# Batch 0's softmax division moved from ScalarE to VectorE and POOL, with new gates on the loads, in a fused attention and squared-ReLU kernel

## The chip, the cores and the metric

The kernel runs on one core of a Trainium2 chip. The metric is the device time of one execution in microseconds. Before the change three runs gave 326.56, 328.07 and 330.91, median 328.07.

## The reference, cut to what matters

```python
scores = scale * np.matmul(q, k.transpose(0, 1, 3, 2))     # B, H, S, D = 4, 8, 768, 64
# mask: own block of 32 and its neighbours, first and last block, 3 sampled blocks a row
scores = np.where(mask, scores, -1000000000.0)
scores = scores - np.max(scores, axis=-1, keepdims=True)
attn = np.exp(scores)
attn = attn / (np.sum(attn, axis=-1, keepdims=True) + 1e-09)
attn_out = np.matmul(attn, v)
x = attn_out.transpose(0, 2, 1, 3).reshape(B * S, H * D)    # 3072 tokens x 512
h = x @ w_in                                                # 512 x 2048
r = np.maximum(h, 0.0)
out = (r * r) @ w_out                                       # 2048 x 512
```

## The kernel before, in words

**Units, slots, groups.** The attention is cut into 16 units `u`, a unit being one pair of heads of one batch (4 units a batch). A unit has 3 query blocks `qi` of 256 queries, and each of them 3 key chunk pairs `cp` of 256 keys. One (u, qi, cp) is a *slot*: TensorE makes the transposed scores of both heads in a PSUM tile `ps` (line 360), ScalarE takes exp into `pT` in bf16 (line 366), and TensorE multiplies `pT` with the values (lines 384 and 386) into `po`. The value tiles `VA` and `VB` carry 64 columns of ones, so that `po` holds the outputs of a head in one half of its partitions and the sums of exp in the other half. The three slots of one (u, qi) are a *group*; there are 48. `po` has one buffer, and so the values of the next group wait until the last reader of the group before is done.

**The division (lines 389 to 405).** After a group's last slot ScalarE takes Ln of the two halves with the sums and Exp of minus that (`inverse`, `ls` and `rs`), and VectorE multiplies outputs and reciprocals into `xT`, one product for each half (`normalize`). These two products are the last readers of `po`.

**The mask.** In batch 0 (u < 4) it is added on TensorE ahead of the scores, as a product of one-hot rows `oh` and a table `bq` (line 356); `bq` comes from `bm`, which VectorE builds from `sampled_blocks` (`sb_i`) at the start, by a product `pb` and one copy of 128x768 on ScalarE (lines 271 to 278). From batch 1 on `pT` is multiplied on VectorE by a 0/1 table `mask` (line 371), which is made in nine pieces during batch 0 (`pq`, lines 280 to 290).

**The feed-forward part.** Batch 0 is worked in 3 tiles of 256 tokens, the others in 2 tiles of 384. For each of 16 blocks `f` of the hidden width TensorE makes `ph` (line 421), VectorE or ScalarE takes the ReLU (`relu_eng` decides; lines 430 and 432), POOL squares it (line 438), and TensorE multiplies with `w_out_sb` into `py` (line 451), which ScalarE copies out (line 456).

**Loads.** Q, K and V come over SP's queue. For batch 0 they are loaded in parts (line 175) and transposed on TensorE. For u of 4 and more, `load(u)` issues three DMAs (line 164), VectorE casts K and POOL casts Q (line 299), and SP issues two DMA transposes (line 321). The weights come over POOL's queue, cast on the way: four pieces of `w_in` (line 335) and four of `w_out` (line 338). A tiny DMA that reads a piece of `w_in` (`loads_gate`, line 342) holds SP's queue until that piece has landed; behind it stand the loads of u = 4 and later.

**What sets the order.** Every engine runs its instructions in the order in which they were issued. That order is made on the host by `run_schedule` (lines 122 to 149): each piece of work is a `Task` with an engine, an assumed duration, a key and what it depends on; the planner takes the task that can start first by these durations, ties by key, and a task behind another on its engine waits with it. Durations, keys, `after` times and gates thus change nothing but the order.

Of the kernel before, what the change touches and what calls it, by code (L numbers as in the profile page):

```python
# [25 lines left out]
def kernel(  # L26
# [136 lines left out]
    def load_part(eng, u, w, c0, c1):  # L166
# [3 lines left out]
        if raw[u][w] is None:  # L170
# [4 lines left out]
        eng.dma_start(out=raw[u][w].rearrange("p t n d -> p t (n d)")[:, :, cols],  # L175
                      in_=(qv, kv, vv)[w][b, a][:, :, cols])

    load_part(nc.scalar, 0, 1, 0, 1)
    load_part(nc.sync, 0, 0, 0, 1)
    sb_i = consts.tile([nb, n_rand * 2], I32, name="sb_i")  # L180
    nc.scalar.dma_start(out=sb_i, in_=sampled_blocks.bitcast(I32))
    load_part(nc.sync, 0, 1, 1, CP)
    load_part(nc.sync, 0, 2, 0, CP)
    load_part(nc.sync, 1, 1, 0, CP)
# [18 lines left out]
    def init_v(eng, i):  # L203
        eng.memset(VA[i][:, :, D:P], 1.0)
        eng.memset(VB[i][:, :, 0:D], 1.0)
# [62 lines left out]
    mask = consts.tile([P, NQ, NCH, QW], BF, name="mask")  # L268
    mtile = {}

    def rows_product():
        pb = ps_s.tile([P, 1024], F32, name="pb", tag="ps")
        nc.tensor.matmul(pb[:, 0:512], bm, oh[0:nb, 0:512], start=True, stop=True)
        nc.tensor.matmul(pb[:, 512:S], bm, oh[0:nb, 512:S], start=True, stop=True)
        mtile["rows"] = pb

    def rows_copy():
        nc.scalar.copy(out=bq, in_=mtile.pop("rows")[:, 0:S])

    def mask_product(qi, cp):  # L280
        pq = ps_y.tile([P, 2, QW], F32, name="pq", tag="y")
# [55 lines left out]
            ns = slice((i - NWP) * NF // NWP, (i - NWP + 1) * NF // NWP)  # L337
            nc.gpsimd.dma_start(out=w_out_sb[:, ns, :], in_=wov[:, ns, :])

    def loads_gate():  # L340

        nc.sync.dma_start(out=scratch, in_=w_in_sb[0:1, 0, (NWP - 1) * d_ff // NWP:(NWP - 1) * d_ff // NWP + 1])


    ptile, stile, otile, rtile, xT = {}, {}, {}, {}, {}
# [1 line left out]
    def scores(slots):  # L347
        for u, qi, cp in slots:
            i = u % NPB
            ps = ps_s.tile([P, 2, 2, QW], F32, name="ps", tag="ps")  # L350
            qsl = slice(qi * QW, (qi + 1) * QW)
            ksl = [slice((cp * 2 + c) * P, (cp * 2 + c + 1) * P) for c in range(2)]
            add = u < HP
            for c in range(2 if add else 0):
                for h, hs in enumerate(HALVES):
                    nc.tensor.matmul(ps[:, h, c, :], oh[hs, ksl[c]], bq[hs, qsl], start=c == 0, stop=False,
                                     skip_group_check=True)
            for c in range(2):
                for h, hs in enumerate(HALVES):
                    nc.tensor.matmul(ps[:, h, c, :], KT[i][hs, ksl[c]], QT[i][hs, qsl], start=not add,  # L360
                                     stop=True, skip_group_check=True)
            stile[u, qi, cp] = ps
# [26 lines left out]
    def inverse(u, qi):  # L389
# [5 lines left out]
        nc.scalar.activation(out=rs, in_=ls, func=AF.Exp, scale=-1.0)  # L395
        rtile[u, qi] = rs

    def normalize(u, qi):
        b, a = divmod(u, HP)
        if b not in xT:  # L400
            xT[b] = consts.tile([P, HP, S], BF, name=f"xT{b}")
        po, rs = otile.pop((u, qi)), rtile.pop((u, qi))
        qsl = slice(qi * QW, (qi + 1) * QW)
        V.tensor_mul(out=xT[b][0:D, a, qsl], in0=po[0:D, 0, :], in1=rs[0:D, :])  # L404
        V.tensor_mul(out=xT[b][D:P, a, qsl], in0=po[D:P, 1, :], in1=rs[D:P, :])  # L405
# [16 lines left out]
                             start=(kc == 0), stop=(kc == KM - 1))  # L422

    def relu_eng(T, f):
        return "ACT" if f % 3 == 2 or (T[0] == 0 and T[1] and f % 3) else "DVE"

    def relu(T, f):
        r = work.tile([P, TWM], F32, name="r", tag="r", bufs=R_BUFS)[:, 0:T[2]]
# [40 lines left out]
            load_part(nc.sync, u, 0, c, c + 1)  # L469
    for i in range(HP):  # L470
        init_v(G, i)

    PT_BUFS, R_BUFS, G_BUFS, QC_BUFS = 9, 4, 2 * NF + 3, 5

    K_PARTS = {0: [(0, 1), (1, CP)]}
# [13 lines left out]
        sc_of[u], va_of[u] = [], []  # L489
    wl, tr, gate, mk, tp = {}, {}, [], {}, {HP - 1: []}  # L490

    rp = Task("PE", 0.5, -7, rows_product, get="ps", **pe)
    rc = Task("ACT", 0.8, -7, rows_copy, deps=[rp], put=[rp], **SEM)
    for qi in range(NQ):
        for cp in range(CP):
            s = HP * CP * NQ + qi * CP + cp - 16
            t = Task("PE", 0.27, s, (lambda a=(qi, cp): mask_product(*a)), deps=[rc],
                     get="y", after=20.0 + 3 * (qi * CP + cp), **pe)
            mk[qi, cp] = Task("DVE", 0.62, s, (lambda a=(qi, cp): mask_copy(*a)), deps=[t], put=[t], **SEM)

    def prepare_first(u):

        tr[u], ev[u] = [], {}
        parts = [(1, c0, c1, t, first[u]) for (c0, c1), t in zip(K_PARTS.get(u, [(0, CP)]), land_k[u])]
        parts += [(0, c, c + 1, land_q[u][c], c * HP * CP + first[u]) for c in range(CP)]
        for w, c0, c1, at, s in parts:
            n = c1 - c0
            a = (u, w, c0, c1)
            on = "POOL" if c0 and not w else "DVE"
            c = Task(on, 0.06 + (0.17 if on == "DVE" else 0.36) * n, s - 6,  # L510
                     (lambda a=a, e=G if on == "POOL" else V: cast_qk(e, *a)), get="qc", after=at, **SEM)
            t = Task("PE", 0.15 * n, s - 5 - w, (lambda a=a: transp(*a)), deps=[c], get="h", put=[c], **pe)
            e = Task("DVE", 0.06 + 0.17 * n, s - 5, (lambda a=a: evac(*a)), deps=[t], put=[t], **SEM)
            tr[u].append(c)
            for i in range(c0, c1):
                ev[u][w, i] = e
        cv[u] = [Task("POOL", 0.6, first[u] - 2, (lambda u=u, h=h: cast_v(u, h)), after=land_v[u], **SEM)
                 for h in range(2)]
        if u == HP - 2:

            for i in range(NWP):
                wl[i] = Task("POOL", 1.0, first[u] + i, (lambda i=i: w_load(i)), deps=cv[u], late=2.0,
                             dma=3.4)
            gate.append(Task("SP", 0.5, 0, loads_gate, deps=[wl[NWP - 1]], late=0.0))

    def prepare(u):
        s0 = first[u]

        ld_t = Task("SP", 1.3, s0 - 20, (lambda u=u: load(u)), deps=cv[u - NRAW] + tr[u - NRAW] + gate,
                    late=2.0, dma=3.9, behind=tp[u - 1])  # L530
        old_sc = sc_of[u - NPB] if u >= NPB else []
        old_va = va_of[u - NPB] if u >= NPB else []
        tr[u], ev[u], tp[u] = [], {}, []
        for w in (1, 0):
            c = Task("DVE" if w else "POOL", 0.6 if w else 1.2, s0 - 12,
                     (lambda w=w: cast_qk(V if w else G, u, w, 0, CP)), deps=[ld_t], get="qc", **SEM)
            t = Task("SP", 1.5, s0 - 12, (lambda w=w: transp_dma(u, w)), deps=[c] + old_sc, put=[c],
                     late=2.0, dma=1.5)
            tr[u].append(c)
            tp[u].append(t)  # L540
            for i in range(CP):
                ev[u][w, i] = t
        early = []
        if u < NPB:
            early = [Task("POOL", 0.8, s0 - 8, (lambda u=u: init_v(G, u)), after=36.0, **SEM)]
        cv[u] = [Task("POOL", 0.6, s0 - 12, (lambda u=u, h=h: cast_v(u, h)), deps=[ld_t] + old_va + early, **SEM)
                 for h in range(2)]
        if u == HP:
            for i in range(NWP, 2 * NWP):
                wl[i] = Task("POOL", 1.0, s0 - 12 + i, (lambda i=i: w_load(i)), deps=cv[u], late=2.0, dma=4.5)  # L550

    N_FIRST = HP * NQ * CP
    N_ONE = 72

    def attend(s, slots):
        sc = Task("PE", 0.42 if len(slots) == 1 and s >= N_FIRST else 0.645, s, (lambda: scores(slots)),
                  deps=[rc] + [ev[u][1, cp] for u, qi, cp in slots] + [ev[u][0, qi] for u, qi, cp in slots] + sc_all[-1:],
                  get="ps", n=len(slots), **pe)
        sc_all.append(sc)
        for j, a in enumerate(slots):  # L560
            u, qi, cp = a
            k = s + j
            ex = Task("ACT", 0.97, k, (lambda a=a: exps(*a)), deps=[sc], get="pT", put=[sc.bufs[j]], **SEM)
            mm = ex
            if u >= HP:
                mm = Task("DVE", 0.82, k - 1, (lambda a=a: mask_mul(V, *a)), deps=[ex, mk[qi, cp]], **SEM)
            va = Task("PE", 0.44, k + 2.2, (lambda a=a: values(*a)), deps=[mm] + cv[u] + va_all[-1:],
                      get=None if cp else "po", put=[ex], **pe)
            va_all.append(va)
            sc_of[u].append(sc)  # L570
            va_of[u].append(va)
            if cp == CP - 1:
                inv = Task("ACT", 1.2, k - 9, (lambda u=u, qi=qi: inverse(u, qi)), deps=[va], **SEM)
                mu[u, qi] = Task("DVE", 0.87, k - 9, (lambda u=u, qi=qi: normalize(u, qi)), deps=[inv],
                                 put=[va_all[-CP]], **SEM)
# [15 lines left out]
    for k, T in enumerate(TILES + [None]):  # L591
# [4 lines left out]
        for _, kind, x in sorted(both, key=lambda e: e[:2]):  # L596
# [15 lines left out]
            else:  # L612
# [9 lines left out]
                if part == NY - 1:  # L622
# [1 line left out]
                              put=[yhead], **SEM)  # L624
                    Task("SP", 0.5, 0, (lambda T_=T_, ts=ts: store(T_, ts)), deps=[yc], put=[yc], late=2.0)

    run_schedule({"PE": 4.9, "DVE": 4.8, "ACT": 3.5, "POOL": 7.5, "SP": 10.5},
                 {"ps": 2, "po": 1, "h": 2, "y": 1, "pT": PT_BUFS, "r": R_BUFS, "g": G_BUFS, "ys": 3,
                  "qc": QC_BUFS}, ring={"SP": 16.0, "POOL": 14.0})

# [29 lines left out]
```

## Time and profile before

| | us |
|---|---|
| median of three runs | 328.07 |
| the profiled execution, its own time | 330.83 |
| its span in the trace | 329.0 |
| TensorE busy (matmuls) | 308.1 |
| ScalarE busy | 229.3 |
| VectorE busy | 197.9 |
| POOL busy | 172.4 |
| mean granted TensorE clock | 0.995 |

A row of a timeline gives the start, the duration, the engine, the line, the operation, what it writes and reads, and in square brackets how long the engine had been idle and what ended that. A row of the waits gives who waited, for whom, the total, the number of waits and the longest. The table of stages gives for each stretch the busy time of each engine and its number of instructions. SPq is SP's DMA queue.

### The profile page before, as it was taken

The page shows a single profiled execution, that of the slowest core. Times are in us where ns is not written, and L with a number is a line of the kernel's source. Part 1 is how long each engine was busy: PE and PEld are TensorE (multiplying, and loading weights), DVE is VectorE, ACT ScalarE, POOL GpSimd, SP SyncE. Part 2 cuts the span into 40 slices and gives each one's busy share as a digit, 9 for nine tenths or more (in the row PEclk, how much of TensorE's full clock was granted, in tenths as well). Part 3 has the DMA queues.
Part 4 walks back from the last instruction along what each step waited for, and adds up shares of the span by engine and source line. Part 5 has one row for each costly group of instructions (what it writes and reads, how often), then busy time and mean ns, then how long its engine had stood idle before and what let it go on. Part 6 is the DMA issues. An engine that isn't in the chain of part 4 may idle for free. (4 is left out here: it accounts for less than half of the span.)

```text
span 329.0 us, 6118 instructions
## 1 busy us (share of the span) xinstructions
PE 308.1 (94%) x2299; PEld 173.8 (53%) x2332; DVE 197.9 (60%) x358; ACT 229.3 (70%) x369; POOL 172.4 (52%) x226
## 2 busy tenths in 40 slices
PE   7989893999999999899999999999999999999994
PEld 2645452655555555455555655555555555555541
DVE  7443542268788687578787775788776764332200
ACT  2799982789799998778787789888778963211111
POOL 7550532287577635178968550356554343665620
PEclk9999999899999999999999999999999999999999
DMA  7997598635563674656061300000000000000002
GB/s 217 335 210 168 106 180 224 181 75 174 169 180 84 194 187 113 192 176 191 2 172 53 81 36 32 2 32 2 32 34 0 33 34 33 34 32 32 34 32 96
DMA packets 42451, 34.47 MB, mean 105 GB/s; under 512 B 20662, under 2 KB 39350, under 8 KB 42422
## 3 DMA queue, kind: packets, MB, share of 16 engines
q1 hardware_dynamic: 37890, 29.76, 31.5%
q0 software_dynamic: 4224, 4.19, 8.0%
q8 instruction: 18, 0.29, 0.4%
q10 hardware_dynamic: 308, 0.13, 0.1%
q14 instruction: 11, 0.09, 0.1%
HBM read 27.26 MB, written 6.29 MB: 102 GB/s over the span
## 5 line engine op out<-in xcount | busy, mean ns | idle before, releaser
L438 POOL TENSOR_TENSOR g<-r 128x384 bf16<-128x384 f32 (+1 forms) x144 | 127.7, 896 | 103.9 <-DVE r L432 76.4
L366 ACT ACTIVATE pT<-ps 128x1024 bf16<-128x1024 f32 x144 | 143.1, 1021 | 37.4 <-PE ps L360 24.1
L421 PE MATMUL ph<-xT,w_in_sb 128*128 128x384 bf16 (+1 forms) x576 | 116.5, 309 | 0.8 <-ACT r L430 0.2
L451 PE MATMUL py<-w_out_sb,g 128*128 128x512 bf16 x351 | 100.5, 379 | 3.6 <-ACT ys L456 2.1
L371 DVE TENSOR_TENSOR pT<-pT,mask 128x1024 bf16<-128x1024 bf16 x108 | 87.1, 820 | 23.7 <-ACT pT L366 21.9
L384 PE MATMUL po<-pT,VA 128*128 128x256 bf16 x288 | 72.3, 278 | 8.5 <-DVE xT L405 5.7
L421 PEld LDWEIGHTS <-w_in_sb 128*128 128x128 bf16 x576 | 53.0, 98 | 44.3 <-issue 10.8
L432 DVE TENSOR_SCALAR r<-ph 128x384 f32<-128x384 f32 (+1 forms) x89 | 46.3, 523 | 49.1 <-PE ph L421 34.4
L386 PE MATMUL po<-pT,VB 128*128 128x256 bf16 x288 | 71.8, 276 | 0.0
L451 PEld LDWEIGHTS <-g 128*128 128x128 bf16 x384 | 37.3, 98 | 27.9 <-issue 2.7
L360 PE MATMUL ps<-QT,KT 64*128 64x256 bf16 x576 | 50.9, 276 | 0.1
L384 PEld LDWEIGHTS <-VA 128*128 128x128 bf16 x288 | 28.2, 98 | 33.8 <-issue 16.8
L430 ACT ACTIVATE r<-ph 128x384 f32<-128x384 f32 (+1 forms) x55 | 23.9, 438 | 26.5 <-POOL g L438 15.9
L360 PEld LDWEIGHTS <-KT 64*128 64x128 bf16 x576 | 22.7, 95 | 20.7 <-issue 18.7
L386 PEld LDWEIGHTS <-VB 128*128 128x128 bf16 x288 | 28.4, 99 | 5.8
L404 DVE TENSOR_TENSOR xT<-po,rs 64x256 bf16<-64x256 f32 x48 | 19.8, 413 | 16.0 <-ACT rs L395 14.8
L299 POOL CAST qc<-qs 128x768 bf16<-128x768 f32 (+1 forms) x20 | 14.4, 727 | 21.1 <-DMA qs<-in_q_dram 19.1
L393 ACT ACTIVATE ls<-po 64x256 f32<-64x256 f32 x48 | 18.3, 382 | 9.9 <-PE po L386 8.9
L456 ACT COPY ys<-py 128x512 f32<-128x512 f32 x24 | 13.9, 584 | 15.2 <-PE py L451 11.4
L395 ACT ACTIVATE rs<-ls 128x256 f32<-128x256 f32 x48 | 20.0, 418 | 1.5
L405 DVE TENSOR_TENSOR xT<-po,rs 64x256 bf16<-64x256 f32 x48 | 20.5, 428 | 0.6
L304 POOL CAST VA<-vs 128x384 bf16<-128x384 f32 x16 | 10.3, 642 | 17.1 <-PE po L384 11.1
(51 smaller groups left out, 112.5 us busy)
## 6 DMA issues: line engine op xcount, KB each, us to landing
vs<-in_v_dram SPq DMA_DIRECT2D x16, 384.0 KB, 5.0
out_dram<-ys SPq DMA_DIRECT2D x24, 256.0 KB, 2.0
ks<-in_k_dram SPq DMA_DIRECT2D x15, 384.0 KB, 4.3
qs<-in_q_dram SPq DMA_DIRECT2D x12, 384.0 KB, 3.6
w_in_sb<-in_moe_w_in_dram POOLq DMA_DIRECT2D x4, 512.0 KB, 9.8
w_out_sb<-in_moe_w_out_dram POOLq DMA_DIRECT2D x4, 512.0 KB, 11.1
qs<-in_q_dram SPq DMA_DIRECT2D x12, 128.0 KB, 6.0
ks<-in_k_dram SPq DMA_DIRECT2D x1, 256.0 KB, 3.3
```

Source lines behind the costliest of these rows:

```text
L360: nc.tensor.matmul(ps[:, h, c, :], KT[i][hs, ksl[c]], QT[i][hs, qsl], start=not add, stop=True, skip_group_check=True)
L366: nc.scalar.activation(out=pT, in_=stile.pop((u, qi, cp)), func=AF.Exp, scale=scale)
L371: eng.tensor_mul(out=pT, in0=pT, in1=mask[:, None, qi, cp * 2:cp * 2 + 2, :].broadcast_to([P, 2, 2, QW]))
L384: nc.tensor.matmul(po[:, 0, :], VA[i][:, n, :], pT[:, 0, c, :], start=first, stop=last, skip_group_check=True)
L386: nc.tensor.matmul(po[:, 1, :], VB[i][:, n, :], pT[:, 1, c, :], start=False, stop=last, skip_group_check=True)
L395: nc.scalar.activation(out=rs, in_=ls, func=AF.Exp, scale=-1.0)
L405: V.tensor_mul(out=xT[b][D:P, a, qsl], in0=po[D:P, 1, :], in1=rs[D:P, :])
L421: nc.tensor.matmul(ph, w_in_sb[:, kc, f * P:(f + 1) * P], xT[b][:, kc, c0:c0 + w], start=(kc == 0), stop=(kc == KM - 1))
L430: nc.scalar.activation(out=r, in_=htile.pop((T, f)), func=AF.Relu)
L432: V.tensor_scalar(out=r, in0=htile.pop((T, f)), scalar1=0.0, scalar2=None, op0=AOP.max)
L438: G.tensor_mul(out=g, in0=r, in1=r)
L451: nc.tensor.matmul(py, gtile[T, f][:, ts * P:(ts + 1) * P], w_out_sb[:, f, :], start=(f == 0), stop=(f == NF - 1))
```

## The change

- At the start `sb_i` is loaded first on SP's queue; the first parts of K and of Q of unit 0 both go over ScalarE's queue.
- The table `bq` is made in three pieces of 256 columns, each with a product of its own in the `y` PSUM buffer and a copy of its own on ScalarE.
- The pieces of `mask` are made in another order and earlier by their keys.
- In batch 0 the 12 groups are divided in another way: four VectorE copies take outputs and sums out of `po` into `ls` and `rs` (`unload`), POOL raises the sums to the power -1 (a tile of -1 as second operand) and multiplies (`divide`). Batches 1 to 3 stay as they were.
- A second gate: after all of `w_out` has landed (u = 5 and later). The first gate reads the last column of `w_in`. The load of u = 5 need no longer stand behind the transposes of u = 4.
- ReLU: the first tile all on VectorE; in the other two tiles of batch 0 every second block on ScalarE (before: two in three); no change in batches 1 to 3.
- Some of the planner's numbers.

`NQ_ADD` is 3, which is `NQ`, so that the additive mask is used where it was before.

```diff
+    sb_i = consts.tile([nb, n_rand * 2], I32, name="sb_i")
+    nc.sync.dma_start(out=sb_i, in_=sampled_blocks.bitcast(I32))
     load_part(nc.scalar, 0, 1, 0, 1)
-    load_part(nc.sync, 0, 0, 0, 1)
-    sb_i = consts.tile([nb, n_rand * 2], I32, name="sb_i")
-    nc.scalar.dma_start(out=sb_i, in_=sampled_blocks.bitcast(I32))
+    load_part(nc.scalar, 0, 0, 0, 1)
...
-    def rows_product():
-        pb = ps_s.tile([P, 1024], F32, name="pb", tag="ps")
-        nc.tensor.matmul(pb[:, 0:512], bm, oh[0:nb, 0:512], start=True, stop=True)
-        nc.tensor.matmul(pb[:, 512:S], bm, oh[0:nb, 512:S], start=True, stop=True)
-        mtile["rows"] = pb
-
-    def rows_copy():
-        nc.scalar.copy(out=bq, in_=mtile.pop("rows")[:, 0:S])
+    def rows_product(qi):
+        pb = ps_y.tile([P, QW], F32, name="pb", tag="y")
+        nc.tensor.matmul(pb, bm, oh[0:nb, qi * QW:(qi + 1) * QW], start=True, stop=True)
+        mtile[qi] = pb
+
+    def rows_copy(qi):
+        nc.scalar.copy(out=bq[:, qi * QW:(qi + 1) * QW], in_=mtile.pop(qi))
...
-    def loads_gate():
-
-        nc.sync.dma_start(out=scratch, in_=w_in_sb[0:1, 0, (NWP - 1) * d_ff // NWP:(NWP - 1) * d_ff // NWP + 1])
+    def loads_gate(n):
+
+        last = w_in_sb[0:1, 0, d_ff - 1:d_ff] if n == 1 else w_out_sb[0:1, NF - 1, 0:1]
+        nc.sync.dma_start(out=scratch, in_=last)
...
-            add = u < HP
+            add = u < HP and qi < NQ_ADD
...
+    def unload(u, qi):
+
+        po = otile.pop((u, qi))
+        et = work.tile([P, QW], F32, name="ls", tag="ls")
+        st = work.tile([P, QW], F32, name="rs", tag="rs")
+        V.tensor_copy(out=et[0:D, :], in_=po[0:D, 0, :])
+        V.tensor_copy(out=st[0:D, :], in_=po[D:P, 0, :])
+        V.tensor_copy(out=et[D:P, :], in_=po[D:P, 1, :])
+        V.tensor_copy(out=st[D:P, :], in_=po[0:D, 1, :])
+        rtile[u, qi] = (et, st)
+
+    def divide(u, qi):
+        b, a = divmod(u, HP)
+        if b not in xT:
+            xT[b] = consts.tile([P, HP, S], BF, name=f"xT{b}")
+        et, st = rtile.pop((u, qi))
+        G.tensor_tensor(out=st, in0=st, in1=minus, op=AOP.pow)
+        G.tensor_mul(out=xT[b][:, a, qi * QW:(qi + 1) * QW], in0=et, in1=st)
...
-        return "ACT" if f % 3 == 2 or (T[0] == 0 and T[1] and f % 3) else "DVE"
+        return "ACT" if (T[0] and f % 3 == 2) or (T[0] == 0 and T[1] and f % 2) else "DVE"
...
+    minus = consts.tile([P, QW], F32, name="minus")
+    V.memset(minus, -1.0)
+
+    NQ_ADD = 3
...
-    rp = Task("PE", 0.5, -7, rows_product, get="ps", **pe)
-    rc = Task("ACT", 0.8, -7, rows_copy, deps=[rp], put=[rp], **SEM)
+    rc = []
+    for qi in range(NQ):
+        rp = Task("PE", 0.2, -7 + 7 * qi, (lambda qi=qi: rows_product(qi)), get="y", **pe)
+        rc.append(Task("ACT", 0.4, -7 + 7 * qi, (lambda qi=qi: rows_copy(qi)), deps=[rp], put=[rp], **SEM))
...
-            s = HP * CP * NQ + qi * CP + cp - 16
-            t = Task("PE", 0.27, s, (lambda a=(qi, cp): mask_product(*a)), deps=[rc],
-                     get="y", after=20.0 + 3 * (qi * CP + cp), **pe)
+            s = HP * CP * NQ_ADD + (qi - 2) % NQ * CP + cp - 6
+            t = Task("PE", 0.27, s, (lambda a=(qi, cp): mask_product(*a)), deps=[rc[qi]],
+                     get="y", after=13.0 + 2.5 * ((qi - 2) % NQ * CP + cp), **pe)
...
-            gate.append(Task("SP", 0.5, 0, loads_gate, deps=[wl[NWP - 1]], late=0.0))
+            gate.append(Task("SP", 0.5, 0, (lambda: loads_gate(1)), deps=[wl[NWP - 1]], late=0.0))
...
-        ld_t = Task("SP", 1.3, s0 - 20, (lambda u=u: load(u)), deps=cv[u - NRAW] + tr[u - NRAW] + gate,
-                    late=2.0, dma=3.9, behind=tp[u - 1])
+        ld_t = Task("SP", 1.3, s0 - 20, (lambda u=u: load(u)), deps=cv[u - NRAW] + tr[u - NRAW] + gate[-1:],
+                    late=2.0, dma=3.9, behind=tp[u - 1] if u > HP + 1 else [])
...
-                wl[i] = Task("POOL", 1.0, s0 - 12 + i, (lambda i=i: w_load(i)), deps=cv[u], late=2.0, dma=4.5)
+                wl[i] = Task("POOL", 1.0, s0 - 12 + i, (lambda i=i: w_load(i)), deps=cv[u], late=2.0, dma=4.0)
+            gate.append(Task("SP", 0.5, 0, (lambda: loads_gate(2)), deps=[wl[2 * NWP - 1]], late=0.0))
...
             if cp == CP - 1:
+                if u < HP:
+                    un = Task("DVE", 1.7, k - 9, (lambda u=u, qi=qi: unload(u, qi)), deps=[va],
+                              put=[va_all[-CP]], **SEM)
+                    mu[u, qi] = Task("POOL", 2.4, k - 9, (lambda u=u, qi=qi: divide(u, qi)), deps=[un], **SEM)
+                    continue
...
-    run_schedule({"PE": 4.9, "DVE": 4.8, "ACT": 3.5, "POOL": 7.5, "SP": 10.5},
+    run_schedule({"PE": 4.4, "DVE": 4.3, "ACT": 3.5, "POOL": 7.5, "SP": 10.5},
```

The diff shows the order only through its rules, so the rows that moved are shown here at two places on VectorE and SP/POOL, with the numbers of the buffers where rows would read alike.

**VectorE, the cast of K of unit 5.** This is the place in batch 0 where VectorE takes K of unit 5 (`ks_789` before, `ks_1230` now) into bf16. Before:

```order
L432 TENSOR_SCALAR r_861<-ph_847 128x256
L289 TENSOR_SCALAR mask_167<-pq_842 128x512
L299 CAST qc_919<-ks_789 128x768
L404 TENSOR_TENSOR xT0_377<-po_856,rs_904 64x256
L405 TENSOR_TENSOR xT0_377<-po_856,rs_904 64x256
L432 TENSOR_SCALAR r_945<-ph_923 128x256
```

Now:

```order
L422 TENSOR_TENSOR xT1_1259<-po_1266,rs_1299 64x256
L423 TENSOR_TENSOR xT1_1259<-po_1266,rs_1299 64x256
L450 TENSOR_SCALAR r_1332<-ph_1310 128x256
L297 CAST qc_1341<-ks_1230 128x768
L450 TENSOR_SCALAR r_1358<-ph_1343 128x256
```

The cast stood between batch 0's groups, ahead of the products of one of them (`xT0`); it now stands behind the second group of unit 4 (`xT1`), after all of batch 0's groups.

**POOL, the loads of `w_out`.** Before, behind the casts of V of unit 4:

```order
L299 CAST qc<-qs 128x768
L304 CAST VA_115<-vs 128x6x64
L304 CAST VB_116<-vs 128x6x64
L338 DMA w_out_sb<-in_moe_w_out_dram 128x4x512 x4
L438 TENSOR_TENSOR g<-r 128x256 x5
```

Now (L413 is the power, L414 the product of `divide`):

```order
L302 CAST VA_115<-vs 128x6x64
L302 CAST VB_116<-vs 128x6x64
L456 TENSOR_TENSOR g<-r 128x256
L413 TENSOR_TENSOR rs<-rs,minus 128x256
L414 TENSOR_TENSOR xT_390<-ls,rs 128x256
L336 DMA w_out_sb<-in_moe_w_out_dram 128x4x512 x2
L413 TENSOR_TENSOR rs<-rs,minus 128x256
L414 TENSOR_TENSOR xT_390<-ls,rs 128x256
L336 DMA w_out_sb<-in_moe_w_out_dram 128x4x512 x2
```

The four loads now stand behind a square and the seventh and eighth of the twelve divisions.

**SP's queue at the same place, now:**

```order
L319 DMA_TRANSPOSE QT_113<-qc 128x6x128
L319 DMA_TRANSPOSE KT_114<-qc 128x6x128
L341 DMA scratch<-w_out_sb 1x1
L163 DMA qs<-in_q_dram 128x2x384
L163 DMA ks<-in_k_dram 128x2x384
L163 DMA vs<-in_v_dram 128x2x384
```

The gate on `w_out` (`scratch`) is new; ahead of it are the transposes of unit 4, behind it the loads of unit 5. Before, those loads followed the transposes directly.

More of the change, by code (lines that the diff above doesn't have):

```diff
@@ L549, in prepare @@
             for i in range(NWP, 2 * NWP):
[L550 to L552 removed]
+                wl[i] = Task("POOL", 1.0, s0 - 12 + i, (lambda i=i: w_load(i)), deps=cv[u], late=2.0, dma=4.0)
+            gate.append(Task("SP", 0.5, 0, (lambda: loads_gate(2)), deps=[wl[2 * NWP - 1]], late=0.0))
+    N_FIRST = HP * NQ_ADD * CP
     N_ONE = 72
@@ L556, in attend @@
         sc = Task("PE", 0.42 if len(slots) == 1 and s >= N_FIRST else 0.645, s, (lambda: scores(slots)),
-                  deps=[rc] + [ev[u][1, cp] for u, qi, cp in slots] + [ev[u][0, qi] for u, qi, cp in slots] + sc_all[-1:],
+                  deps=[rc[qi] for u, qi, cp in slots if qi < NQ_ADD and u < HP] + [ev[u][1, cp] for u, qi, cp in slots] + [ev[u][0, qi] for u, qi, cp in slots] + sc_all[-1:],
                   get="ps", n=len(slots), **pe)
@@ L564, in attend @@
             mm = ex
-            if u >= HP:
+            if u >= HP or qi >= NQ_ADD:
                 mm = Task("DVE", 0.82, k - 1, (lambda a=a: mask_mul(V, *a)), deps=[ex, mk[qi, cp]], **SEM)
```

## The prediction

> **What bounds the kernel now.** First the busy times of the whole page, then the same by stages, since the shares of the whole are a mean over stages with different limits.
>
> ```profile
> span 329.0 us, 6118 instructions
> PE 308.1 (94%) x2299; PEld 173.8 (53%) x2332; DVE 197.9 (60%) x358; ACT 229.3 (70%) x369; POOL 172.4 (52%) x226
> ```
>
> ```profile
> core 0: us, PE busy (x) PEld busy (x) DVE busy (x) ACT busy (x) POOL busy (x), PEclk, DMA share, GB/s
> 16.00:48.00 32.00, 29.11 (x313) 16.80 (x311) 15.89 (x36) 29.06 (x42) 13.37 (x25) 1.00 0.93 166
> 48.00:60.00 12.00, 7.01 (x53) 3.90 (x53) 1.85 (x5) 5.09 (x8) 2.01 (x3) 0.87 0.89 203
> 60.00:72.00 12.00, 11.87 (x108) 6.97 (x109) 5.62 (x12) 10.04 (x18) 7.10 (x11) 0.99 0.40 118
> 72.00:120.00 48.00, 47.27 (x381) 27.58 (x387) 38.47 (x63) 44.01 (x78) 32.39 (x44) 1.00 0.56 154
> ```
>
> TensorE has work for 308.1 of 329.0 us, and the change takes no matmul away (one is added, a third `pb`). So it can only win TensorE's idle time, or make more of it. From 72 to 120 us TensorE is idle for 0.73 us: nothing to win there. The change touches batch 0, and batch 0 holds two sources of idle time. From 16 to 48 us TensorE loses 32.00 - 29.11 = 2.89 us, and ScalarE is as busy as TensorE, 29.06 us. From 48 to 60 us TensorE loses 12.00 - 7.01 = 4.99 us, and there no engine is busy; something holds them all. The waits of batch 0 and the timelines of VectorE, SP and TensorE at this place name it:
>
> ```profile
> PE po L384 <- DVE xT L405: 4.9, 1, 4.9
> DVE qc L299 <- DMA ks<-in_k_dram: 7.6, 1, 7.6
> ```
>
> ```profile
> 46.95 0.68 DVE L289 TENSOR_SCALAR mask<-pq 128x512 bf16<-128x512 f32 x1
> 55.25 0.56 DVE L299 CAST qc<-ks 128x768 bf16<-128x768 f32 x1 [7.62 <-DMA ks<-in_k_dram]
> 55.72 0.41 DVE L404 TENSOR_TENSOR xT<-po,rs 64x256 bf16<-64x256 f32 x1
> 56.15 0.43 DVE L405 TENSOR_TENSOR xT<-po,rs 64x256 bf16<-64x256 f32 x1
> ```
>
> ```profile
> 41.10 0.89 SPq L164 DMA_DIRECT2D ks<-in_k_dram  x1
> ```
>
> ```profile
> 56.63 0.28 PE L384 MATMUL po<-pT,VA 128*128 128x256 bf16 x1 [4.94 <-DVE xT L405]
> 57.35 0.61 PE L356 MATMUL ps<-bq,oh 64*128 64x256 bf16 x4
> 60.00 0.42 PE L384 MATMUL po<-pT,VA 128*128 128x256 bf16 x1
> ```
>
> VectorE reached the cast of K of unit 5 at about 47.6 us, and this K, issued at 41.10, landed 14 us later. Behind the cast stood the two products that free `po`; TensorE's next values needed `po` and came at 56.63. K was late because the four loads of `w_out` were on the same DMA engines:
>
> ```profile
> 35.97 3.29 POOL L338 DMA_DIRECT2D w_out_sb<-in_moe_w_out_dram  x4
> DMA to landing us min/median/max: 6.3/11.1/15.6
> DMA to landing us min/median/max: 3.1/4.4/14.1
> ```
>
> The second row is of `w_out`, the third of the loads of line 164: 4.4 us is their median, 14.1 us the worst, and the worst is here. Unit 5 comes after the nine slots of unit 4, whose first scores are these (no mask product of line 356 ahead of them):
>
> ```profile
> 66.56 0.39 PE L360 MATMUL ps<-QT,KT 64*128 64x256 bf16 x4
> ```
>
> So this is a wait of an in-order queue for data that was needed more than ten us later, not a bound of an engine.
>
> **The change, part by part.** The sum is made against the profiled execution (span 329.0, its own time 330.83). Its difference is then taken off the median 328.07, which lies 2.8 us below the profiled one; 2% of the median is 6.6 us, about what a measurement of this kernel can tell from no change.
>
> *The wait at 51.7 us goes.* As the order shows, VectorE now casts K of unit 5 after all of batch 0's groups and two groups of unit 4, and SP issues that load only after `w_out` has landed, when nothing competes with it. Removed: the 4.94 us. Removed with it: after the pause four matmuls take 0.61 us (row at 57.35) where the same four take 0.39 with a warm clock:
>
> ```profile
> 60.48 0.39 PE L356 MATMUL ps<-bq,oh 64*128 64x256 bf16 x4
> ```
>
> From 56.9 to 60.2 us that ratio costs 3.3 x (1 - 0.39 / 0.61) = 1.2 us; I take 1.0, since some rows of that stretch are short already. Sum -5.9; the bounds are 0 (it turns up elsewhere, below) and -6.1.
>
> *ScalarE is relieved.* Each group loses Ln, Ln and Exp:
>
> ```profile
> L393 ACT ACTIVATE ls<-po 64x256 f32<-64x256 f32 x10 | 3.8, 382 | 0.4 <-PE po L386 0.2
> L394 ACT ACTIVATE ls<-po 64x256 f32<-64x256 f32 x10 | 3.8, 377 | 0.1
> L395 ACT ACTIVATE rs<-ls 128x256 f32<-128x256 f32 x10 | 4.2, 418 | 0.3
> L366 ACT ACTIVATE pT<-ps 128x1024 bf16<-128x1024 f32 x38 | 37.7, 1019 | 14.2 <-PE po L386 10.0 <-PE ps L360 3.8
> ```
>
> 0.382 + 0.377 + 0.418 = 1.18 us, times 12 groups 14.1 us. A group costs ScalarE 3 x 1.02 + 1.18 = 4.24 us now and 3.06 then. But TensorE was itself busy for 29.11 of these 32 us: at most its 2.89 us can be won. I take two thirds, -1.9; bounds 0 and -2.9. The rest of the 14.1 us is off the path.
>
> *VectorE takes more.* Four copies of 64x256 out of PSUM stand for two products of the same size. There is no row of such a copy; the nearest are the products themselves and a ReLU of 128x256 out of PSUM:
>
> ```profile
> L404 DVE TENSOR_TENSOR xT<-po,rs 64x256 bf16<-64x256 f32 x9 | 3.7, 416 | 4.2 <-ACT rs L395 4.2
> L405 DVE TENSOR_TENSOR xT<-po,rs 64x256 bf16<-64x256 f32 x9 | 3.8, 428 | 0.1
> L432 DVE TENSOR_SCALAR r<-ph 128x256 f32<-128x256 f32 x10 | 4.1, 422 | 6.6 <-PE ph L421 3.4 <-POOL VB L304 3.1
> ```
>
> All three give 0.42 us, so 4 x 0.42 = 1.68 us in place of 0.84, and 12 x 0.84 = 10.1 us more. ReLUs also come over from ScalarE: 5 in the first tile (all 16 on VectorE in place of 11) and 2 in each of the two others (8 in place of 6), 9 x 0.42 = 3.8 us. VectorE is idle for 16.1 + 10.2 + 6.4 = 32.7 us from 16 to 72 us, so 13.9 us fit. What is late, when they do not fit at the place, is the mask products and ReLUs of unit 4, which now stand among the copies: I add +0.5; bounds 0 and +3.
>
> *POOL takes the division.* A power and a product of 128x256 for each group. The product is priced by the squares, the power has no row. The nearest ones, from batch 0 and from the start:
>
> ```profile
> L438 POOL TENSOR_TENSOR g<-r 128x256 bf16<-128x256 f32 x13 | 8.1, 630 | 13.2 <-DVE r L432 7.9 <-ACT r L430 5.1
> masks.py:199 POOL TENSOR_SCALAR_AFFINE_SELECT identb<-identb 128x128 bf16<-128x128 bf16 x1 | 0.6, 583 | 0.1
> ```
>
> Below, a power cannot be cheaper than a product: pair 2 x 0.63 = 1.26 us. The dearest POOL row a column is the select, 583 ns for 128 columns, which makes 1.17 us for 256 and a pair of 1.8 us. Nothing in the trace closes it above. POOL is idle for 56 - (13.37 + 2.01 + 7.10) = 33.5 us from 16 to 72 us, and 12 pairs fit as long as one is below 33.5 / 12 = 2.8 us. I take 1.8 and count 0, hidden by that idle time; the price without cover is among the rivals. Behind a late division stand, on POOL, the squares and the `w_out` loads; on VectorE the copies of the group after next, since `ls` and `rs` have two buffers; and behind those TensorE's values.
>
> *`w_out` and unit 5 later.* `w_out` now waits for the seventh and eighth division. The Ln of the seventh group stands in the trace at
>
> ```profile
> 49.09 0.38 ACT L393 ACTIVATE ls<-po 64x256 f32<-64x256 f32 x1
> ```
>
> With ScalarE relieved I put it 4 us earlier, at 45, and the loads of `w_out` at 46 to 51. With 11.1 us to landing they are in at 62; then 4.4 us for unit 5, about 1 for the cast and 2.8 for each of two transposes, one after the other: 73 us. From some 60 us, when by my estimate unit 4's scores are mostly out (they begin 8 us or more ahead of the row at 66.56), TensorE has the values of unit 4 and hidden products to do without unit 5:
>
> ```profile
> 45.00 0.61 PE L421 MATMUL ph<-xT,w_in_sb 128*128 128x256 bf16 x4
> KT<-qc SPq DMA_TRANSPOSE x5, 2.8
> ```
>
> A tile of 256 tokens has 64 of these matmuls, 16 x 0.61 = 9.8 us, and two such tiles are open by then. That covers 60 to 73, if their ReLUs and squares keep up: +0.5; bounds 0 and +5.
>
> *The start.* The first parts of K and Q are cast at 5.70 and 6.39, the copy of `bq` takes 0.80, and the first exp runs at 8.76:
>
> ```profile
> 6.68 0.80 ACT L278 CAST bq<-pb 128x768 bf16<-128x768 f32 x1 [3.40 <-PE pb L274]
> 8.76 1.94 ACT L366 ACTIVATE pT<-ps 128x1024 bf16<-128x1024 f32 x2 [1.28 <-PE ps L360]
> ```
>
> A third of that copy is ready about 0.4 us earlier, and Q is cast ahead of the second part of K. But `sb_i` was waited for 0.3 us only, so its new queue wins little. -0.6; bounds 0 and -1.2.
>
> Sum: -5.9 - 1.9 + 0.5 + 0 + 0.5 - 0.6 = -7.4 us. 328.07 - 7.4 = 320.7 us; the profiled span would be 321.6.
>
> **Rivals.**
>
> *The wait moves (20%).* A gate replaces one wait with another: SP's queue stands at `w_out`, and everything after, unit 5's loads and the later ones, is late by it. For it: my cover from 60 to 73 us rests on an estimate, and ScalarE, with nothing but ReLUs and copies to do meanwhile, has its exps pushed into 72 to 120 us, where it is already busy for 44.01 of 48. Against it: the feed-forward products can fill TensorE. Price: the 5 us bound in place of 0.5, so -7.4 + 4.5 = -2.9, 325.2 us.
>
> *The power costs four products (6%).* 4 x 0.63 = 2.5, pair 3.15 us, 0.35 beyond what fits; 12 x 0.35 = 4.2 us late, 324.9 us. The Trainium skill (GPSIMD Engine Reference, section 3.1) states that data-dependent branching costs about 12 cycles an element there at 1.2 GHz; if a power is such a body, an estimate by that page is 256 x 12 / 1.2 = 2.56 us. No run here shows it.
>
> *The power is dear, and POOL becomes the bound (14%): slower.* Place: `divide` in batch 0, POOL in order. From a pair of 2.8 us on it eats the gain; at 2.8 + 7.4 / 12 = 3.4 us nothing is left; at 2.8 + (7.4 + 6.6) / 12 = 4.0 us it is slower by 2%. At 4.5 us: 12 x 1.7 = 20.4 us late, 320.7 + 20.4 = 341 us. For it: no row bounds a power from above, and the squares and loads of `w_out` stand in the same queue. Against it: the two elementwise POOL rows above lie at 0.58 and 0.63 us.
>
> *The wait is not in most executions.* The profiled one is the slowest of the three, 2.8 us above the median; if that is the wait, the median has only 3.1 of its 5.9 us to give, and the result is 323.5 us. That lies in the forecast's own range and has no chance of its own.
>
> **How the numbers follow.** The forecast has 60%, with a range of its own from 316.5 (all gains at their bounds, -6.1 - 2.9 - 1.2 = -10.2, make 317.9, and a run can lie 1.5 us below its median, as 326.56 does) to 324. Faster by over 2% is below 321.5: I give it 50 of the 60. Within 2% are the other 10 and both rivals of 20 and 6. Slower has 14. The range for 8 in 10 reaches from 316.5 through the rivals of 325 into the dear power, to 331; left out are about 1 in 10 above and less below.
>
> **What would show it.** Right: no wait of `po` L384 of over 2 us in batch 0; the cast of K of unit 5 not waiting on a DMA; first exp before 8.4 us; rows of the power at 1.0 to 2.2 us; four copies at 0.42 each; ScalarE below 26 us from 16 to 48. Wrong: a power over 2.2 us, VectorE's copies waiting on POOL, a stretch of several us around 60 to 80 in which TensorE waits for K or Q of unit 5, or a wait for `xT` on the hidden products of the first tile.

## The result, and the profile after

The changed kernel took 790.84 us (median of 4 runs, 788.82 to 791.64), the kernel before 329.49 in the runs beside it: 2.406 times as long, 95% interval 2.385 to 2.427. (This ratio and those below leave out slow executions of the kernel before, over 1.5% above its fastest, and so differ a little from the ratio of the medians.) I had forecast 320.7 us with a range to 331.0, and given 14% to any slowing down. The profiled execution took 790.15 us, its span is 788.4.

The busy times of the whole page, after:

```profile
span 788.4 us, 6178 instructions
PE 331.8 (42%) x2333; PEld 184.0 (23%) x2333; DVE 211.5 (27%) x392; ACT 215.3 (27%) x326; POOL 677.8 (86%) x250
```

TensorE went from 94% of the span to 42%, POOL from 52% to 86%. The costliest group of instructions is new, and it is one line:

```profile
L413 POOL TENSOR_TENSOR rs<-rs,minus 128x256 f32<-128x256 f32 x12 | 495.9, 41323 | 2.2 <-DVE rs L405 2.2
```

The power takes 41.3 us. I had put it at 1.17, from a select of 128 columns. Twelve of them are 495.9 us. POOL's timeline at the first, and at the last:

```profile
17.08 41.37 POOL L413 TENSOR_TENSOR rs<-rs,minus 128x256 f32<-128x256 f32 x1 [2.15 <-DVE rs L405]
58.53 0.73 POOL L414 TENSOR_TENSOR xT<-ls,rs 128x256 bf16<-128x256 f32 x1
59.20 0.51 POOL L302 CAST VA<-vs 128x384 bf16<-128x384 f32 x1
```

```profile
494.65 41.68 POOL L413 TENSOR_TENSOR rs<-rs,minus 128x256 f32<-128x256 f32 x1
536.40 0.72 POOL L414 TENSOR_TENSOR xT<-ls,rs 128x256 bf16<-128x256 f32 x1
```

Everything that POOL has to do in batch 0 stands between the powers: here a cast of V at 59.20 that waits for nothing but its turn. The table of stages, cut at the first power and the last product, shows POOL full in all of that time and nobody else:

```profile
17.00:537.00 520.00, 74.18 (x514) 38.81 (x511) 38.72 (x86) 40.19 (x42) 518.92 (x52) 0.55 0.07 13
537.00:789.00 252.00, 242.57 (x1708) 137.36 (x1707) 161.48 (x268) 166.47 (x274) 148.08 (x170) 0.99 0.31 90
```

(The columns are stretch and its length, then busy time and number of instructions of PE, PEld, DVE, ACT and POOL, then the granted clock of TensorE, the share of the DMA engines and GB/s.) The waits from 17 to 537 us name the way from POOL to the rest:

```profile
ACT pT L365 <- PE po L385: 274.6, 12, 83.8
DVE ls L402 <- POOL xT L414: 223.3, 6, 41.3
PE po L383 <- DVE rs L405: 143.2, 4, 37.4
```

Read from the second row: VectorE's copies for the group after next wait until POOL has given a buffer of `ls` and `rs` back, up to 41.3 us, one power; TensorE's values wait for those copies to free `po`; ScalarE's exps wait for TensorE's values to free `pT`. The granted clock of 0.55 is a companion, not a cause: TensorE had 74 us of work in 520.

### The profile page after: what moved, and what is told of

Same layout as the page of the kernel before. It is cut to its first block, busy times and chain, and to the rows that moved or that the text cites. A ratio compares the mean times of both kernels' runs of the same rounds, so it can differ in the third digit from the quotient of the medians.

```text
span 788.4 us, 6178 instructions
## 1 busy us (share of the span) xinstructions
PE 331.8 (42%) x2333; PEld 184.0 (23%) x2333; DVE 211.5 (27%) x392; ACT 215.3 (27%) x326; POOL 677.8 (86%) x250
## 5 line engine op out<-in xcount | busy, mean ns | idle before, releaser
L413 POOL TENSOR_TENSOR rs<-rs,minus 128x256 f32<-128x256 f32 x12 | 495.9, 41323 | 2.2 <-DVE rs L405 2.2
L439 PE MATMUL ph<-xT,w_in_sb 128*128 128x384 bf16 (+1 forms) x576 | 124.8, 318 | 145.1 <-DVE r L450 111.9
L469 PE MATMUL py<-w_out_sb,g 128*128 128x512 bf16 x384 | 111.6, 384 | 83.2 <-POOL g L456 81.8
L383 PE MATMUL po<-pT,VA 128*128 128x256 bf16 x288 | 80.9, 303 | 145.8 <-DVE rs L405 143.2
L450 DVE TENSOR_SCALAR r<-ph 128x384 f32<-128x384 f32 (+1 forms) x98 | 50.2, 514 | 221.0 <-POOL g L456 169.5
L385 PE MATMUL po<-pT,VB 128*128 128x256 bf16 x288 | 80.5, 301 | 0.0
L402 DVE COPY ls<-po 64x256 f32<-64x256 f32 x12 | 5.0, 416 | 232.2 <-POOL xT L414 223.3
L359 PE MATMUL ps<-QT,KT 64*128 64x256 bf16 x576 | 54.7, 292 | 0.5 <-ACT pT L365 0.4
L392 ACT ACTIVATE ls<-po 64x256 f32<-64x256 f32 x36 | 13.7, 380 | 91.5 <-PE po L385 90.9
L308 PE MATMUL pt<-identb,qc 128*128 128x128 bf16 x48 | 6.2, 264 | 76.1 <-POOL qc L297 76.1
L448 ACT ACTIVATE r<-ph 128x384 f32<-128x384 f32 (+1 forms) x46 | 20.7, 451 | 33.0 <-POOL g L456 20.6
```

Source lines behind the costliest of these rows:

```text
L383: nc.tensor.matmul(po[:, 0, :], VA[i][:, n, :], pT[:, 0, c, :], start=first, stop=last, skip_group_check=True)
L385: nc.tensor.matmul(po[:, 1, :], VB[i][:, n, :], pT[:, 1, c, :], start=False, stop=last, skip_group_check=True)
L413: G.tensor_tensor(out=st, in0=st, in1=minus, op=AOP.pow)
L439: nc.tensor.matmul(ph, w_in_sb[:, kc, f * P:(f + 1) * P], xT[b][:, kc, c0:c0 + w], start=(kc == 0), stop=(kc == KM - 1))
L448: nc.scalar.activation(out=r, in_=htile.pop((T, f)), func=AF.Relu)
L450: V.tensor_scalar(out=r, in0=htile.pop((T, f)), scalar1=0.0, scalar2=None, op0=AOP.max)
```

## The experiments

**The power against a product.** The power is replaced by a product of the same two operands; nothing else differs, and the order is the same. The reciprocal is left out.

```diff
-        G.tensor_tensor(out=st, in0=st, in1=minus, op=AOP.pow)
+        G.tensor_tensor(out=st, in0=st, in1=minus, op=AOP.mult)
```

> The changed kernel with the power replaced by a product of the same operands (the reciprocal is left out, so the division is not computed); order, loads, gates and copies are those of the change. Theory A (the power's own duration, 41.24 us twelve times on POOL's in-order queue, is all of the loss): the time falls to 316.5 to 324 us, my forecast's own range, since the pair is then 2 x 0.63 to 0.73 us and fits POOL's idle time; no wait of po above 2 us in batch 0. Theory B (the new order and gates lose time by themselves): above 335 us. In between, 324 to 330: the power is the loss, but the gains that I summed to -7.4 are not there.

Measured: 320.47 us (319.20 to 321.65), 0.980 of before, interval 0.972 to 0.988. Theory A holds and B falls. The last product of the divisions now starts at 65.0 us and takes 1.05; from there to the end of the span of 317.4 us are 251.4 us. With the power the last product ended at 537.1, and from there to the end at 788.4 are 251.3 us. What follows batch 0 is the same length; all of the difference lies in front of it.

**What the power costs by.** Twelve shapes and values in one kernel, a different one in each group, to separate a price a column, a price an element, a start-up and a dependence on values. The other reciprocals are left out.

```diff
-        G.tensor_tensor(out=st, in0=st, in1=minus, op=AOP.pow)
+        n = qi * HP + a
+        if n == 0:
+            G.tensor_tensor(out=st, in0=st, in1=minus, op=AOP.pow)
+        elif n == 1:
+            G.tensor_tensor(out=st[:, 0:128], in0=st[:, 0:128], in1=minus[:, 0:128], op=AOP.pow)
...
+        elif n == 5:
+            G.tensor_tensor(out=st[0:8, :], in0=st[0:8, :], in1=minus[0:8, :], op=AOP.pow)
+        elif n == 6:
+            G.tensor_tensor(out=st, in0=one, in1=minus, op=AOP.pow)
+        elif n == 7:
+            G.tensor_tensor(out=st, in0=st, in1=one, op=AOP.pow)
...
+        else:
+            V.reciprocal(out=st, in_=st)
```

> One look at the duration of the power in twelve shapes, one in each group (the rest of each group's reciprocals is left out, so the output is not the reference's). In order of the groups: 128x256; 128x128; 128x64; 64x256; 16x256; 8x256; 128x256 with base 1.0; 128x256 with exponent 1.0; 1x256; 32x256; 128x16; VectorE's reciprocal of 128x256 from SBUF. Theory A1 (a fixed cost a column of the instruction, 161 ns): 41.2, 20.7, 10.4, 41.2, 41.2, 41.2, 41.2, 41.2, 41.2, 41.2, 2.7 us. Theory A2 (each element by itself, a core's 16 partitions one after the other): 16x256 is 41.2 as well, 8x256 half of it, 20.6, and 1x256 2.6 us. Theory A3 (most of it is a start-up, a code load for instance): the narrow ones stay near 41 us, or the first is longer than the rest. Theory A4 (the values matter): base 1.0 or exponent 1.0 is far below 41 us.

POOL's timeline of this kernel, the powers alone in order of time:

```profile
18.52 41.38 POOL L415 TENSOR_TENSOR rs<-rs,minus 128x256 f32<-128x256 f32 x1 [2.78 <-DVE rs L405]
63.48 20.82 POOL L417 TENSOR_TENSOR rs<-rs,minus 128x128 f32<-128x128 f32 x1
87.13 10.54 POOL L419 TENSOR_TENSOR rs<-rs,minus 128x64 f32<-128x64 f32 x1
98.43 41.22 POOL L421 TENSOR_TENSOR rs<-rs,minus 64x256 f32<-64x256 f32 x1
140.41 41.22 POOL L423 TENSOR_TENSOR rs<-rs,minus 16x256 f32<-16x256 f32 x1
183.86 41.22 POOL L425 TENSOR_TENSOR rs<-rs,minus 8x256 f32<-8x256 f32 x1
227.31 41.23 POOL L427 TENSOR_TENSOR rs<-one,minus 128x256 f32<-128x256 f32 x1
270.88 41.28 POOL L429 TENSOR_TENSOR rs<-rs,one 128x256 f32<-128x256 f32 x1
314.51 41.25 POOL L431 TENSOR_TENSOR rs<-rs,minus 1x256 f32<-1x256 f32 x1
358.24 41.67 POOL L433 TENSOR_TENSOR rs<-rs,minus 32x256 f32<-32x256 f32 x1
401.81 2.91 POOL L435 TENSOR_TENSOR rs<-rs,minus 128x16 f32<-128x16 f32 x1
```

Theory A1, a price a column, holds in all of them. From 128 to 256 columns the price rises by 20.6 us, 0.16 us a column, and 16 columns at 2.91 us leave about 0.3 us that do not depend on the width. One partition costs as much as 128, base 1.0 and exponent 1.0 cost as much as the sums and -1, and the first is no longer than the rest: A2, A3 and A4 fall. The estimate of 2.56 us that I had made by the Trainium skill (GPSIMD Engine Reference, section 3.1: about 12 cycles an element for data-dependent branching) is 16 times too low for this body; the measurement decides. VectorE's reciprocal of 128x256 took 1.74 us. (The kernel ran once and took 664.87 us.)

**Does the price that I had put on a dear power hold?** The power on 16 columns only, which the last row prices at 2.91 us (the other reciprocals are left out):

```diff
-        G.tensor_tensor(out=st, in0=st, in1=minus, op=AOP.pow)
+        G.tensor_tensor(out=st[:, 0:16], in0=st[:, 0:16], in1=minus[:, 0:16], op=AOP.pow)
```

> The changed kernel with the power on 16 of 256 columns only (the other reciprocals are left out). The power then takes 2.91 us by the look at its shapes, the pair 3.63. By the prediction's price of a dear power, 12 x (3.63 - 2.8) = 10 us on top of 320.5: 330.5 us. If POOL's idle time is worth less than I counted (order instead of sums decides): 340 us or more. If it is worth more: 321 to 325 us.

Measured: 331.00 us (10 runs), 1.006 of before, interval 1.001 to 1.012, where 330.5 was expected. Its power's row and its stage from 16 to 72 us:

```profile
L413 POOL TENSOR_TENSOR rs<-rs,minus 128x16 f32<-128x16 f32 x12 | 36.7, 3056 | 2.2 <-DVE rs L405 2.1
```

```profile
16.00:72.00 56.00, 47.31 (x475) 28.18 (x474) 33.27 (x76) 36.90 (x38) 53.05 (x47) 0.94 0.67 129
```

POOL is full, 53.05 of 56 us, and the time rises. The twelve pairs cost 26.1 us more than with the product (36.7 - 9.2 for the power, and 8.7 in place of 10.1 for the products), of which 10.5 reach the end: POOL's idle time took the rest, as the break-even of 2.8 us a pair said.

**The division of before under the new order.** The new tasks are taken out, so that `inverse` and `normalize` work in batch 0 as well:

```diff
-                if u < HP:
-                    un = Task("DVE", 1.7, k - 9, (lambda u=u, qi=qi: unload(u, qi)), deps=[va],
-                              put=[va_all[-CP]], **SEM)
-                    mu[u, qi] = Task("POOL", 2.4, k - 9, (lambda u=u, qi=qi: divide(u, qi)), deps=[un], **SEM)
-                    continue
```

> The changed kernel with the division of before in batch 0 (Ln, Ln, Exp on ScalarE, two products on VectorE); load order, pieces of bq, mask order, gates and ReLU split are the change's. If the wait at 51.7 us was the main prize and the gate takes it: 328 - 5.9 - 0.6 + 0.5, about 322 us. If the division on other engines was what would have brought the gain: no better than before, 327 to 331 us. If the new gates only move the wait: 326 us or more, with TensorE waiting for unit 5 between 60 and 80 us.

Measured: 323.61 us (321.98 to 324.86), 0.988, interval 0.978 to 0.998. That is 1.6 us above the first of my expectations and clear of the second: the rest of the change gains without the new division. Its stages from 16 us on:

```profile
16.00:48.00 32.00, 28.71 (x311) 16.29 (x309) 15.80 (x37) 29.00 (x41) 12.25 (x23) 1.00 0.76 140
48.00:60.00 12.00, 11.85 (x120) 7.35 (x121) 4.39 (x11) 10.12 (x16) 3.59 (x6) 1.00 0.89 156
```

The stall is gone (11.85 of 12 us, 7.01 before). The idle time beside the busy ScalarE is not (28.71 of 32 us, 29.11 before).

**The gates alone,** on the kernel before (the function of the gate and the planner's 4.0 for a piece of `w_out` come with them):

```diff
+            gate.append(Task("SP", 0.5, 0, (lambda: loads_gate(2)), deps=[wl[2 * NWP - 1]], late=0.0))
...
-        ld_t = Task("SP", 1.3, s0 - 20, (lambda u=u: load(u)), deps=cv[u - NRAW] + tr[u - NRAW] + gate,
-                    late=2.0, dma=3.9, behind=tp[u - 1])
+        ld_t = Task("SP", 1.3, s0 - 20, (lambda u=u: load(u)), deps=cv[u - NRAW] + tr[u - NRAW] + gate[-1:],
+                    late=2.0, dma=3.9, behind=tp[u - 1] if u > HP + 1 else [])
```

> The kernel before with nothing but the load gates of the change (gate on all of w_in, second gate on w_out, the load of unit 5 free of unit 4's transposes, 4.0 for a w_out piece in the planner). If the 4.9 us wait at 51.7 us is removed by the gates: 328.1 to 329.8 less 5.9, 322 to 324 us, and the table of stages shows TensorE above 11 of 12 us from 48 to 60. If gates only move the wait: 327 to 330 us.

Measured: 325.21 us (324.43 to 325.47), 0.986, interval 0.979 to 0.994; 1 us above what I expected. The stall is gone here too:

```profile
48.00:60.00 12.00, 11.89 (x114) 7.26 (x113) 3.69 (x9) 10.39 (x18) 3.52 (x6) 1.00 0.76 177
120.00:160.00 40.00, 36.36 (x280) 21.04 (x282) 30.92 (x52) 32.74 (x53) 23.00 (x25) 1.00 0.51 148
```

The second row shows where a part is given back: from 120 to 160 us TensorE is busy for 36.36 us, where it had 37.93 before. The rival that the wait is not in most executions is not settled, since only one trace of the kernel before was kept. The times hint at it: the executions of the kernel before that count in this ratio lie from 326.6 to 331.5 us, the four with the gates from 324.4 to 325.5.

**The new division alone,** with a product for the power (reciprocal left out), on the kernel before: `unload`, `divide` and their tasks as in the change, nothing else.

> The kernel before with the new division alone and a product for the power (reciprocal left out); loads, gates, bq, mask order and ReLU split as before. By my terms only ScalarE's 1.9 us, less 0.5, are won and the wait for K of unit 5 stays: 326 to 329 us. If the division is what carries the gain: 321 to 323 us, with no wait of po on a DMA.

Measured: 323.95 us (323.37 to 324.55), 0.983, interval 0.975 to 0.991. This is better than I expected, and my expectation was wrong in what it said of the stall. VectorE's, SP's and POOL's timelines of this kernel:

```profile
51.24 0.55 DVE L299 CAST qc<-ks 128x768 bf16<-128x768 f32 x1
```

```profile
43.26 0.47 SPq L164 DMA_DIRECT2D ks<-in_k_dram  x1
```

```profile
46.54 2.28 POOL L338 DMA_DIRECT2D w_out_sb<-in_moe_w_out_dram  x3
```

The cast of K of unit 5 waits for nothing. The divisions in POOL's queue push the loads of `w_out` back to 46.54 us, behind unit 5's loads, while before they went out at 35.97, ahead of them. The new division thus takes the stall away a second time, by what it holds up, but it gives a part back in the next stage, where TensorE had been busy for 11.87 us:

```profile
48.00:60.00 12.00, 10.51 (x104) 6.79 (x101) 9.23 (x19) 8.01 (x9) 8.33 (x12) 1.00 1.12 178
60.00:72.00 12.00, 8.73 (x75) 5.20 (x76) 11.84 (x20) 8.97 (x14) 11.14 (x13) 1.00 0.79 159
```

**A reciprocal on VectorE,** in the place of the copy of the sums:

```diff
-        V.tensor_copy(out=st[0:D, :], in_=po[D:P, 0, :])
+        V.reciprocal(out=st[0:D, :], in_=po[D:P, 0, :])
...
-        G.tensor_tensor(out=st, in0=st, in1=minus, op=AOP.pow)
```

> The power is taken away and VectorE's copy of the sums out of PSUM becomes a reciprocal out of PSUM (same number of VectorE instructions), POOL keeps the product. If a reciprocal of 64x256 costs what a copy costs (0.42 us), the time is that of the kernel with the product, 316.5 to 324 us. If it costs 8 passes, 8 x 256 / 0.96 GHz as a guess of the same kind that failed for the power, 2.1 us or more each, VectorE gets 24 x 1.7 = 41 us more in batch 0 where it has 33 us idle: 330 us or more.

Measured: 361.00 us (359.33 to 361.63), 1.103, interval 1.094 to 1.112. One of the two reciprocals, and the wait that goes with it:

```profile
L403 DVE RECIPROCAL rs<-po 64x256 f32<-64x256 f32 x12 | 21.1, 1759 | 0.2
```

```profile
PE po L383 <- DVE rs L405: 24.3, 11, 3.1
```

1.76 us a reciprocal, 4.2 times a copy and below the 2.1 of the worse of my two cases. By this price VectorE has 24 x 1.34 = 32 us more to do, which its idle time of 33 us would just have held, and still 40 us are lost on the kernel with the product. I read it from the waits: `po` is held for 4.4 us a group in place of 1.7, and 11 of 12 groups make TensorE wait. The granted clock is lower too, 0.81 from 16 to 48 us, so that a part of the loss is slower matmuls. All of that is argued, not tried by itself.

**Ln and Exp out of SBUF.** The experiments say: keep the early unloading and the gates, and take the reciprocal where it is cheap. Two activations of 128x256 on the unloaded sums stand in the place of the power:

```diff
+    def invert(u, qi):
+        et, st = rtile[u, qi]
+        nc.scalar.activation(out=st, in_=st, func=AF.Ln)
+        nc.scalar.activation(out=st, in_=st, func=AF.Exp, scale=-1.0)
+
...
-        G.tensor_tensor(out=st, in0=st, in1=minus, op=AOP.pow)
...
-                    mu[u, qi] = Task("POOL", 2.4, k - 9, (lambda u=u, qi=qi: divide(u, qi)), deps=[un], **SEM)
+                    inv = Task("ACT", 0.85, k - 9, (lambda u=u, qi=qi: invert(u, qi)), deps=[un], **SEM)
+                    mu[u, qi] = Task("POOL", 0.85, k - 9, (lambda u=u, qi=qi: divide(u, qi)), deps=[inv], **SEM)
```

> The changed kernel with the power replaced by ScalarE's Ln and Exp on the unloaded sums, both 128x256 out of SBUF (0.42 us each, 0.84 a group in place of 1.18 before), as a task of its own in the planner; VectorE still frees po with four copies and POOL still makes the product. It computes the reference. If early unloading and the gates carry the gain of the kernel with the product (320.47 us), 321 to 323 us, better than the old division under the same gates (323.61). If relieving ScalarE carried it, 10.1 of the 14.1 us come back to ScalarE and it is no better than 323.6.

Measured: 318.73 us (318.05 to 319.31), 0.967 of before, interval 0.958 to 0.977. It computes the whole reference and is the fastest of all. Its activations and two of its stages:

```profile
L410 ACT ACTIVATE rs<-rs 128x256 f32<-128x256 f32 x12 | 5.0, 416 | 3.2 <-DVE rs L405 3.2
L411 ACT ACTIVATE rs<-rs 128x256 f32<-128x256 f32 x12 | 5.0, 416 | 0.4
```

```profile
16.00:48.00 32.00, 31.70 (x349) 18.80 (x348) 21.98 (x51) 29.78 (x41) 16.02 (x29) 1.00 0.74 139
48.00:60.00 12.00, 11.95 (x116) 7.41 (x115) 9.14 (x21) 10.64 (x15) 7.35 (x12) 1.00 0.94 169
```

That is 2.3 us below the 321 that I had expected at best, and 4.9 us below the old division under the same gates (323.61). TensorE is busy for 31.70 of 32 us with ScalarE as busy as before (29.78, 29.06). But what won TensorE these 2.9 us is not shown, since two things changed together. `po` is freed by the copies, ahead of any Ln. And a division costs ScalarE 2 x 0.416 = 0.83 us in place of 1.18, which for the 6 or 7 groups of this stretch makes 2.1 to 2.4 us; ScalarE takes 27 exps in it, where it took 23 before. In the kernel before, TensorE's matmuls wait in this stretch for exps and not for `po` (only two of its weight loads do, for 1.6 us together), which speaks for the second:

```profile
PE ps L356 <- ACT pT L366: 1.5, 2, 0.8
PE po L384 <- ACT pT L366: 1.1, 2, 0.7
```

My expectation cannot decide it either: it set 10.1 us that come back to ScalarE against a gain that was never above 2.9. The planner's order differs too, since its prices do; that share was not separated.

## Why the prediction was wrong, point by point

**The step that failed** is the price in *POOL takes the division*: "The dearest POOL row a column is the select, 583 ns for 128 columns, which makes 1.17 us for 256 and a pair of 1.8 us. Nothing in the trace closes it above. [...] I take 1.8". Measured: 41.3 us and a pair of 42.0. The second failure follows from the first: with no row that closed the price above, I still ended the range at 331, gave the open side 14% and worked it out for a pair of 4.5 us, as if an unknown operation could lie no further off.

**The mechanism behind the price was right.** The rival named the place (`divide`, POOL in order), the chain (`ls` and `rs` with two buffers, VectorE's copies, TensorE's values), and the rule of 12 times what a pair takes beyond 2.8 us. With 42.0 us this rule gives 320.7 + 12 x (42.0 - 2.8) = 791 us; 790.84 were measured. With 3.78 us (3.06 and 0.72) it gives 332.5; 331.00 were measured. The kernel with twelve shapes is a third point: its eleven powers, each with a product of 0.72, lie 341.9 us beyond 2.8 a pair, which makes 662.6; 664.87 were measured. That the first comes out to the microsecond is luck in part: the 2.8 comes from POOL's idle time in three stages of the kernel before.

**The other terms,** read in the kernel with the product, whose 320.47 us stand against the forecast of 320.7. Its stages, and its first exps:

```profile
16.00:48.00 32.00, 31.89 (x349) 18.80 (x348) 21.57 (x52) 25.30 (x26) 18.84 (x33) 1.00 0.63 126
48.00:60.00 12.00, 10.25 (x97) 6.60 (x94) 7.56 (x19) 8.59 (x9) 9.23 (x13) 1.00 1.01 163
60.00:72.00 12.00, 10.00 (x81) 7.05 (x82) 11.39 (x22) 5.22 (x9) 11.31 (x14) 1.00 0.30 100
```

```profile
7.57 2.86 ACT L365 ACTIVATE pT<-ps 128x1024 bf16<-128x1024 f32 x3 [0.59 <-PE ps L359]
```

- The stall: gone, as forecast, but TensorE wins 10.25 - 7.01 = 3.2 us there and not the 4.9 of the wait. Of the 1.75 us that are left, 1.5 are four waits for exps to free `ps` (first row below). In the kernels with the old division under the new order, with the gates alone and with Ln and Exp, TensorE is busy for 11.85 to 11.95 us there.
- ScalarE: 25.30 us from 16 to 48, below the 26 that I had set, and TensorE's idle time there falls from 2.89 to 0.11 us. I had 1.9. Whether ScalarE's load was the reason stays open, as said of the kernel with Ln and Exp.
- Copies on VectorE: 0.42 us each, as priced.
- Unit 5 later: from 60 to 72 us TensorE is idle for 2.0 us where it was 0.13 before. I had +0.5 of a bound of 5. But 1.6 of it is one wait of unit 4's values for a product on VectorE (second row below), which is busy for 11.39 of these 12 us; TensorE waits nowhere here for K or Q of unit 5. So by these rows most of the loss belongs to the term *VectorE takes more*, for which I had +0.5 of a bound of 3.
- The start: the first exp at 7.57 in place of 8.76. That is the far bound of my -0.6, but it does not hold: in the trace of the changed kernel, with the same start, the first exp is at 8.38, and in those of the gates alone and of the division alone, with the old start, at 8.28 and 8.12.

```profile
PE ps L359 <- ACT pT L365: 1.5, 4, 0.5
PE po L383 <- DVE xT L423: 1.6, 1, 1.6
```

That 320.47 meets 320.7 is therefore luck in part. TensorE's idle time up to 72 us falls from 10.25 to 6.28 us, by 4.0, while the span falls by 11.6 (329.0 to 317.4; the medians by 7.6 from 328.07, by 9.4 in the same round). The place is right: by 72 us TensorE's rows show 647 matmuls, 568 before, and 79 of them at the mean of 0.131 us (302.0 / 2301) are, by this estimate, 10.4 us. But the part that is not idle time, more matmuls in about the same busy time, is in no term of mine, and no run shows its cause.

## What to carry to other kernels

An operation without a row in any trace, on an in-order engine with many instances in series, is measured by itself before the kernel is built on it; until then the range stays open on that side, and the break-even price (here 2.8 us a pair) is the number to hold on to. Price it by its slope over columns and partitions, not by its neighbours on the engine. And a total that meets the forecast does not show that its terms were right. Copies that free `po` early, with Ln and Exp on the unloaded sums, gave 318.73 us; whether the early release or the lighter ScalarE did it has to be separated by a run of its own.

## What the runs showed of the hardware that I had not expected

- POOL's float power costs 0.16 us a column and about 0.3 us beside it, whatever the number of partitions (1 to 128) and for all the values tried (the sums and 1.0, exponents -1 and 1); a product of 128x256 takes 0.72 us in the same place, 57 times less.
- VectorE's reciprocal takes 1.76 us for 64x256 out of PSUM and 1.74 us for 128x256 out of SBUF, 4.2 times a copy of 64x256 (0.42 us).
